# First layer norm of a transformer block: the transposes of tiles 8 to 15 move from TensorE to the DMA queue, and the order of work is planned anew

## The chip, the cores and the metric

One core of a Trainium2 chip. Its engines work in parallel, each through a list of instructions of its own, in order: PE (TensorE, matmuls), ACT (ScalarE), DVE (VectorE), POOL (GpSimd) and SP (SyncE, which issues nearly all DMAs here). An instruction waits at the head of its list until the semaphores that it names have come up, and all behind it wait too. The metric is the device time of one execution in microseconds, the median of several runs. The profile is one more execution, recorded instruction by instruction; its times count from the start of the recorded span.

## The reference

One adaptive layer-norm transformer block over 2048 tokens of width 1024: attention with 32 query heads that share one key and one value head of width 32, then a gated feed-forward layer of width 3584. Cut to what is computed:

```python
mod = (silu(c) @ w_mod).reshape(1, 6, 1, -1)
sa, ca, ga, sb, cb, gb = (mod[:, i] for i in range(6))
h = layernorm(x) * (1 + ca) + sa
q = heads(h @ wq)                       # 32 heads of width 32
k, v = h @ wk, h @ wv                   # one head each
p = softmax(q @ k.T * 32 ** -0.5)
x = x + ga * (concat(p @ v) @ wo)
h = layernorm(x) * (1 + cb) + sb
x = x + gb * ((silu(h @ w1) * (h @ w3)) @ w2)
```

## The kernel before

The tokens are cut in 16 tiles of 128 (index `tt`) and in 8 blocks of 256 (index `n`). TensorE contracts over partitions, so the normed input must lie with its features on partitions: that is `HT`, 128 x 8 x 2048, and the first norm fills it tile by tile.

**First norm, `lnt1(tt)`.** Per tile: two statistics instructions and an aggregation on VectorE (`ST`, `MV`), two or three tiny instructions on GpSimd (`RS`, `NB`), then the norm itself into one of three slots `XN[tt % 3]` (`XNB` 0, `XNB` 1 and a slice of `PS`), on ScalarE for tiles 0 to 7 and on VectorE from tile 8 on. Then TensorE transposes the slot in eight 128 x 128 pieces into a PSUM bank, and ScalarE or VectorE (whichever the planner picks) copies the bank into `HT`. A slot can be written again when its transposes are done. Tiles 6 to 15 of x lie in the buffer `W2S`.

**Projections.** `k_proj(j)` takes `HT` tiles 2j and 2j+1, eight matmuls, and its result goes into `KT` part j (by VectorE or ScalarE). `v_proj(tb)` takes four tiles, 32 small matmuls. `q_proj` fills `QT`. `mod_chunk(i)` loads 1 MB of `w_mod` into one of two buffers inside `W2S` and multiplies it with silu(c).

**Attention.** One step c stands for block n, query group f (of 8) and key part j (of 8): `s_exp(c)` issues 8 score matmuls (S) on TensorE and two exponentials on ScalarE (U<-S), each 128 x 1024. There are 512 steps, so 1024 exponentials. Step c of the first row (c = 0 to 7) needs `KT` part c. `av` multiplies U with V and sums the denominators; `wo` adds the attention output to x and takes the second norm; `slab` and `quarter` are the feed-forward layer (a tanh on ScalarE per slab). In the second norm of blocks 1 to 6 the transposes are already done by DMA, SBUF to SBUF (`wo`, `dma_start_transpose` from `XN` into `QT`).

**Order.** Nothing above fixes the order on an engine. `Graph` collects the operations with their dependencies, a due time `vt` and an estimated duration; `Placer.run` then simulates the engines, and picks at each point among the operations that are ready. `PLAN` has one row for 16 steps: tolerances, and offsets to the due times by kind and engine (`"k/dve"`). What `Placer` picks becomes the fixed list of each engine. `Placer.commit` books the estimated end of an operation. For a DMA it books one shared queue, `self.bw`: a transfer starts when the earlier ones are through, takes `nbytes / n.bw`, and ends 0.5 later in the planner's account.

**The lists around the change, before.** e3 is one of the two exponentials of step 3, S3 its matmuls, T and N the transposes and the norm of a tile, H its copy into `HT`, k4 the matmuls of `k_proj(4)`, KT4 its eviction. From the first exponential on:

```
ACT: e0 e0 e1 e1 H11 e2 e2 e3 KT5 H12 e3 e4 H13 e4 H14 e5 H15 e5 e6 KT7 e6 e7 e7 ...
PE:  S0 q T9 S1 T10 k2 T11 S2 k3 k4 S3 k5 T12 S4 qbias T13 S5 T14 k6 T15 vbr S6 v0 k7 v1 S7 v2 v3 S8 ...
DVE: ... N11 QT H9 H10 KT2 ... KT3 KT4 N12 ... N13 ... N14 ... N15 KT6 ...
SP:  ... x(8-11) w_mod w_mod wq x(12-15) WO WO w_mod(0) w_mod(1) ...
```

T8 stands on TensorE ahead of S0, and H8 on ScalarE ahead of e0. SP's load of WO waits until wq has landed.

Of the kernel before, what the change touches and what calls it, by code (L numbers as in the profile page):

```python
# [8 lines left out]
P = 128  # L9
# [33 lines left out]
class Graph:  # L43
# [63 lines left out]
    def alias(self, new, old):  # L107
# [5 lines left out]


PLAN = [
    (0.2, 0.03, 0.0, 0, 1.4,
     {"q/pe": -9, "slab/act": -80, "wo/dve": -71, "ln/pe": -112, "ln/act": 31, "k/pe": 3, "k/dve": 33}),
    (0.0, 0.12, 0.2, 1, 0.2,
     {"av/pe": -2, "q/pe": -9, "pair/dve": -2, "av/dve": -33, "slab/act": -18, "ln/pe": -57, "ln/act": 23}),
    (0.0, 0.16, 0.02, 0, 0.7, {"wo/pe": 106, "q/pe": -45, "q/dve": -74, "ln/pe": -118, "ln/dve": 4, "mod/pe": -24}),  # L120
    (0.0, 0.16, 0.02, 0, 0.7, {"wo/pe": 106, "q/pe": -45, "q/dve": -74, "ln/pe": -118, "ln/dve": 4, "mod/pe": -24}),
    (0.2, 0.24, 0.2, 1, 0.6, {"q/pe": 47, "mc/pe": 46, "ln/act": -12, "k/pe": 22}),
    (0.0, 0.12, 0.2, 0, 1.8,
     {"wo/pe": -44, "quarter/pe": 47, "q/pe": 33, "mc/pe": 36, "pair/dve": -14, "wo/dve": -1, "ln/act": -12,
      "k/pe": 22}),
    (0.0, 0.11, 0.2, 1, 1.5, {"q/pe": 47, "mc/pe": 46, "av/dve": 6, "ln/act": -12, "k/pe": 22}),
    (0.0, 0.11, 0.2, 1, 1.9, {"q/pe": -13, "mc/pe": 46, "av/dve": 4, "ln/act": -12, "k/pe": 22}),
    (0.0, 0.11, 0.2, 0, 3.4, {"wo/pe": 35, "an/dve": 55, "slab/dve": 1}),
    (0.0, 0.11, 0.2, 1, 1.4, {"av/dve": -11, "an/dve": 55, "slab/dve": 1, "q/dve": 9}),
    (0.0, 0.11, 0.1, 0, 2.4,  # L130
     {"wo/pe": 14, "slab/pe": 12, "quarter/pe": 3, "q/pe": -6, "av/dve": 18, "an/dve": 69, "slab/act": -1,
      "quarter/dve": -7}),
    (0.0, 0.11, 0.05, 0, 2.4, {"slab/act": 6, "wo/dve": 53}),
    (0.0, 0.11, 0.2, 0, 2.9, {"wo/pe": 46, "an/dve": 55, "slab/dve": -89, "q/dve": 67}),
    (0.0, 0.11, 0.2, 1, 1.3, {"wo/pe": -13, "pair/dve": 6, "an/dve": 55, "slab/dve": -89, "q/dve": 67}),
    (0.0, 0.11, 0.1, 1, 2.7,
# [16 lines left out]
     {"wo/pe": 112, "slab/pe": -124, "quarter/pe": 26, "q/pe": 20, "mc/pe": 46, "pair/dve": 13, "av/dve": -89,  # L153
      "an/dve": -26, "slab/dve": -39, "slab/act": -20, "quarter/dve": 35, "wo/dve": -2, "ln/act": -12,
      "k/pe": 22}),
    (0.0, 0.11, 0.2, 1, 1.3,
     {"slab/pe": -124, "quarter/pe": 26, "q/pe": 52, "mc/pe": 46, "pair/dve": 13, "av/dve": -72, "an/dve": -26,
      "slab/dve": -39, "slab/act": -20, "quarter/dve": 35, "wo/dve": -6, "ln/act": -12, "k/pe": 22}),
    (0.0, 0.11, 0.05, 1, 2.6,
     {"slab/pe": -124, "quarter/pe": 26, "q/pe": 20, "mc/pe": 46, "av/dve": -89, "slab/dve": -39,  # L160
      "slab/act": -20, "quarter/dve": 35, "ln/act": -12, "k/pe": 22}),
    (0.0, 0.11, 0.05, 1, 1.4,
     {"slab/pe": -124, "quarter/pe": 26, "q/pe": 20, "mc/pe": 5, "av/dve": -89, "slab/act": -20,
      "quarter/dve": 35, "ln/act": -12, "k/pe": 22}),
    (0.0, 0.11, 0.2, 0, 1.6, {"wo/pe": 74, "pair/dve": 40, "av/dve": -2, "an/dve": 55, "slab/dve": -102, "q/dve": 6}),
    (0.0, 0.11, 0.2, 1, 1.4, {"wo/pe": -13, "pair/dve": 40, "av/dve": -2, "an/dve": 55, "slab/dve": -88}),
    (0.0, 0.11, 0.05, 1, 1.9,
# [19 lines left out]
class Placer:  # L187
# [121 lines left out]
    def commit(self, n, e, k, start):  # L309
        eng, fn, dur = n.alts[k]  # L310
        e = eng
        s = n.sess
        if s is not None and s.bank is None:
            bt, b = self.bank_for(n)
            s.bank = b
            s.prev = self.bank_of[b][1]
            self.bank_of[b] = None
            for p in s.prev:
                n.preds.setdefault(p, False)
        n.eng = e  # L320
        if e == "sp" or n.dma is not None:
            self.t[e] = start + dur
            self.bw = max(self.bw, start + 2.6) + n.nbytes / n.bw
            n.fin = self.bw + 0.5
        else:
            if e == "dve" and n.tag in ("pair", "av"):
                self.lock = start + dur
            if e == "pool" and self.lock > start:
                dur = max(dur, self.lock - start + (0.43 if dur > 0.5 else 0.1))
            self.t[e] = start + dur  # L330
            n.fin = start + dur + n.post + self.SEM
        if e == "pe":
            if s is not None and n.mode == "F":
                s.fill = any(not x.done and x is not n and x.alts[0][0] == "pe" for x in s.nodes)
                if s.fill:
                    self.fills.add(s)
                else:
                    self.fills.discard(s)
            if n.mode == "S":
                self.step += 1  # L340
            self.mode = n.mode
            if n.mode != "S":
                self.run_of = n.mode
            else:
                self.t_s = self.t["pe"]
        n.done = True
        if s is not None:
            s.left -= 1
            if s.left == 0:
                users = [x for x in s.nodes if x.eng != "pe"] or [s.nodes[-1]]  # L350
                self.bank_of[s.bank] = (max(x.fin for x in users), tuple(users))
        self.emit(n, e, fn)
        self.free_pending()
# [90 lines left out]
def build(nc, x_in, wq_in, wk_in, wv_in, wo_in, w1_in, w3_in, w2_in, c_in, wmod_in, out, S, D, F):  # L444
    G = Graph(nc)
    op = G.op
    NC = D // P
# [21 lines left out]
    HT = sb("HT", [P, NC, S], BF16)  # L469
# [38 lines left out]
    XN = [XNB[:, 0], XNB[:, 1], PS[:, 5].rearrange("p h q -> p (h q)")]  # L508
    o = 0
# [19 lines left out]
    def xtile(tt):  # L529
        if tt < 6:  # L530
            return X1[:, tt // 2, tt % 2, :]
        return W2f[:, (tt - 6) * D:(tt - 5) * D]

    def xkey(tt):
        return [("X", tt // 2, tt % 2, q) for q in range(4)] if tt < 6 else [("XS", tt)]
# [56 lines left out]
    def wq_dma(f0, f1, key, vt):  # L592
# [18 lines left out]
       writes=["C1"], vt=-1990)  # L611
    op("dve", lambda: [lambda e: e.tensor_scalar(SCC[:, 2, :], SCC[:, 1, :], 0.5, 0.5, ALU.mult, ALU.add)], 0.17,
       reads=["C1"], writes=["C2"], vt=-1990)
    op("dve", lambda: [lambda e: e.tensor_tensor(SCC[:, 3, :], SCC[:, 2, :], SCC[:, 0, :], ALU.mult)], 0.17,
       reads=["C0", "C2"], writes=["C3"], vt=-1990)
# [11 lines left out]
    for i in range(2):  # L627
# [3 lines left out]
           writes=[("S", 4)], vt=-1990, mode="F", post=0.145, waw=(i == 0))  # L631
# [5 lines left out]
       reads=[("WKV", 0)], writes=["WKR0"], vt=-1600)  # L637
# [13 lines left out]
    def ln_norm(xap, tt, keys, slot, vt):  # L651
        op("dve", lambda: [lambda e: e.tensor_scalar(XN[slot], xap, MV[:, tt, 0:1], RS[:, tt:tt + 1],
                                                     ALU.subtract, ALU.mult)], 0.455,
           reads=keys + [("MV", tt), ("RS", tt)], writes=[("XN", slot)], vt=vt)

    def lnt1(tt, vt):
        G.tag = "ln"
        slot = tt % 3
        xap = xtile(tt)
        ln_stats(xap, tt, xkey(tt), vt)  # L660
        if tt < 8:
            op("pool", lambda: [lambda e: e.tensor_scalar(NB_[:, tt:tt + 1], MV[:, tt, 0:1], RS[:, tt:tt + 1], -1.0,
                                                          ALU.mult, ALU.mult)], 0.3, reads=[("MV", tt), ("RS", tt)],
               writes=[("NB", tt)], vt=vt)
            op("act", lambda: [lambda e: e.activation(XN[slot], xap, ACT.Identity, bias=NB_[:, tt:tt + 1],
                                                      scale=RS[:, tt:tt + 1])], 1.15,
               reads=xkey(tt) + [("RS", tt), ("NB", tt)], writes=[("XN", slot)], vt=vt)
        else:
            ln_norm(xap, tt, xkey(tt), slot, vt)
        static = tt < 6  # L670
        s = None if static else Sess()
        bk = [("S", tt)] if static else [("sess", id(s), tt)]

        def tr(b=tt):
            return [lambda e, cc=cc: e.transpose(
                BANKH[b][:, cc * P:(cc + 1) * P], XN[slot][:, cc * P:(cc + 1) * P],
                IDENT[:]) for cc in range(NC)]
# [547 lines left out]
```

## Time and profile before

| what | us |
|---|---|
| median of 3 runs (lowest, highest) | 1134.34 (1134.11, 1134.49) |
| profiled execution, its own time | 1134.47 |
| its span | 1132.6 |
| PE busy | 1113.1 |
| ACT busy | 1026.0 |
| DVE busy | 951.9 |
| POOL busy | 53.8 |
| first exponential starts | 30.61 |
| ACT idle, 300 to 400 / 400 to 500 | 0 / 1.4 |

The busy time of an engine is the union of its instructions' times; matmuls overlap, so a busy TensorE is not one at its peak. A group's line names the output tile, the input tiles, shapes and count, then busy us and mean ns of one, then the engine's idle us just before such instructions and who ended it. In a timeline the columns are start, length, engine, instruction; neighbours of one kind are merged, with their count at the end. The granted TensorE clock was 1.00 in all stretches.

### The profile page before, as it was taken

How to read it: one execution, taken by the hardware profiler on the slowest of the kernel's cores; microseconds unless marked ns; L12 is line 12 of the kernel's file. 1: busy time of each engine (PE TensorE's matmuls, PEld its weight loads, DVE VectorE, ACT ScalarE, POOL GpSimd, SP SyncE). 2: the span in 40 equal slices, each digit the busy share in tenths (PEclk: the TensorE clock that was granted, in tenths of full speed). 3: DMA queues.
4: the chain of work that ended last, by engine and by line, in shares of the span. 5: the costliest groups of instructions: out<-in, count | busy, mean ns of one | idle time of the engine just before them, and what ended most of it. 6: DMA issues, size and time to landing. Idle time of an engine off the chain costs nothing.

```text
span 1132.6 us, 34805 instructions
## 1 busy us (share of the span) xinstructions
PE 1113.1 (98%) x15600; PEld 754.6 (67%) x15600; DVE 951.9 (84%) x1544; ACT 1026.0 (91%) x1165; POOL 53.8 (5%) x95
## 2 busy tenths in 40 slices
PE   7999999999999999999999999999999999999998
PEld 6643546666577656776567756776577657766887
DVE  7888899989988888888988998888988988888442
ACT  6999999999999999999999999999999999996110
POOL 5100000000100001000100000000100000000000
PEclk9999999999999999999999999999999999999999
DMA  9500379665596667766596658765696559667793
GB/s 344 184 2 1 114 225 242 186 196 151 129 263 194 173 166 209 208 191 165 141 262 192 174 148 237 196 193 142 173 248 195 160 146 238 190 185 209 217 296 116
DMA packets 374292, 209.47 MB, mean 185 GB/s; under 512 B 17536, under 2 KB 365952, under 8 KB 374144
## 3 DMA queue, kind: packets, MB, share of 16 engines
q1 hardware_dynamic: 373712, 207.11, 65.8%
q8 instruction: 123, 2.02, 0.8%
q14 instruction: 25, 0.20, 0.1%
q10 hardware_dynamic: 432, 0.13, 0.0%
HBM read 199.89 MB, written 4.19 MB: 180 GB/s over the span
## 4 chain that ended last, share of the span: by engine, by line
PE 63%; ACT 31%; DVE 4%; DMA 1%; issue 0%; POOL 0%; SPq 0%; DVEq 0%
PE PB L22 47%; ACT U L22 30%; PE S L22 16%; DVE PS L22 2%; DMA W<-in_A_wq_dram 1%; ACT HT L22 1%; DVE HT L22 1%; DVE RB L22 0%; SPq L22 0%; DVE ST L22 0%; DVE W L22 0%; ACT XNB L22 0%; POOL PS L22 0%; DVE XNB L22 0%; POOL RS L22 0%
## 5 line engine op out<-in xcount | busy, mean ns | idle before, releaser
L22 ACT ACTIVATE U<-S 128x1024 bf16<-128x1024 f32 x1024 | 964.3, 1111 | 9.0 <-PE S L22 8.8
L22 DVE TENSOR_TENSOR PS<-U 128x2048 bf16<-128x2048 bf16 x256 | 309.7, 1214 | 11.7 <-ACT U L22 10.3
L22 DVE TENSOR_TENSOR PS<-PS 128x1024 bf16<-128x1024 bf16 x368 | 249.5, 684 | 4.7
L22 PE MATMUL PB<-QT,W 128*128 128x256 bf16 x1856 | 229.6, 273 | 0.0
L22 PE MATMUL S<-QT,KT 32*128 32x256 bf16 x4096 | 203.5, 273 | 6.0 <-ACT U L22 4.0
L22 PEld LDWEIGHTS PB<-QT,W 128*128 128x128 bf16 x1856 | 170.3, 98 | 46.6 <-issue 28.3
L22 PE MATMUL PB<-W2S,HT 128*128 128x256 bf16 x1512 | 189.1, 273 | 0.0
L22 PEld LDWEIGHTS PB<-W2S,HT 128*128 128x128 bf16 x1512 | 137.5, 98 | 42.4 <-issue 26.4
L22 PEld LDWEIGHTS S<-QT,KT 32*128 32x128 bf16 x4096 | 60.8, 92 | 132.7 <-ACT U L22 118.7
L22 PE MATMUL PB<-U,V 128*32 128x256 bf16 x4032 | 123.5, 273 | 0.0
L22 PE MATMUL PB<-QT,HT 128*128 128x256 bf16 x960 | 119.9, 273 | 0.0
L22 PEld LDWEIGHTS PB<-U,V 128*32 128x32 bf16 x4032 | 100.8, 97 | 18.8 <-issue 7.0
L22 ACT ACTIVATE HT<-PB 128x512 bf16<-128x512 f32 (+1 forms) x110 | 77.6, 707 | 32.0 <-PE PB L22 31.8
L22 PEld LDWEIGHTS PB<-QT,HT 128*128 128x128 bf16 x960 | 88.2, 98 | 23.7 <-issue 14.1
L22 PE MATMUL PB<-HT,W 128*128 128x256 bf16 (+1 forms) x576 | 101.8, 318 | 1.0 <-DVE HT L22 0.6
L22 DVE SCALAR_TENSOR_TENSOR HT<-HT,PB 128x512 bf16<-128x512 bf16 x102 | 69.4, 681 | 34.2 <-ACT HT L22 33.4
L22 DVE TENSOR_TENSOR HT<-HT,PB 128x512 bf16<-128x512 bf16 x102 | 69.5, 681 | 19.2 <-PE PB L22 18.5
L22 PEld LDWEIGHTS PB<-HT,W 128*128 128x128 bf16 x576 | 49.9, 97 | 38.1 <-issue 15.2
L22 DVE STREAM_TRANSPOSE RB<-PB 128x256 f32<-128x256 f32 x63 | 28.2, 448 | 38.7 <-PE PB L22 38.5
L22 PE MATMUL PB<-WO,QT 128*128 128x512 bf16 x232 | 57.3, 381 | 0.0
L22 POOL TENSOR_SCALAR RS<-MV 128x1 f32<-128x1 f32 x32 | 10.5, 329 | 969.9 <-DVE MV L22 966.9
L22 ACT ACTIVATE HT<-S 128x512 bf16<-128x512 f32 (+1 forms) x15 | 10.9, 736 | 30.5 <-PE S L22 30.5
(115 smaller groups left out, 675.2 us busy)
## 6 DMA issues: line engine op xcount, KB each, us to landing
W<-in_B_w_dram SPq DMA_DIRECT2D x150, 512.0 KB, 4.8
W2S<-in_B_w_dram SPq DMA_DIRECT2D x28, 1792.0 KB, 8.6
HT<-in_B_w_dram SPq DMA_DIRECT2D x74, 512.0 KB, 4.8
W2S<-in_w_mod_dram SPq DMA_DIRECT2D x8, 1024.0 KB, 7.2
X<-in_A_x_dram SPq DMA_DIRECT2D x8, 512.0 KB, 7.0
out_dram<-X SPq DMA_DIRECT2D x7, 512.0 KB, 9.1
U<-in_B_w_dram SPq DMA_DIRECT2D x1, 3584.0 KB, 13.5
W2S<-in_B_w_dram SPq DMA_DIRECT2D x1, 3584.0 KB, 15.2
```

The costliest lines, as they stand in the source:

```text
L22: return getattr(e, call[0])(*call[1], **call[2])
```

## The change

In `lnt1`, tiles 8 to 15 leave the function early: in place of eight TensorE transposes, a PSUM bank and a copy there is one `dma_start_transpose` on SP, from the norm's slot straight into `HT`. Its rate is given as a negative number, and `Placer.commit` has a branch for it: such a transfer neither waits for the shared queue `self.bw` nor adds to it. Tiles 0 to 7 stay as they were. `PLAN` has new values in rows 0 to 11 and in two later rows, so the lists of all engines differ in many places.

```diff
-    (0.2, 0.03, 0.0, 0, 1.4,
-     {"q/pe": -9, "slab/act": -80, "wo/dve": -71, "ln/pe": -112, "ln/act": 31, "k/pe": 3, "k/dve": 33}),
...
+    (0.0, 0.15, 0.1, 0, 2.9,
+     {"slab/pe": -44, "q/pe": 25, "mc/pe": 25, "slab/dve": -38, "slab/act": -18, "wo/dve": -95, "ln/pe": -112,
+      "ln/act": 172, "k/dve": 33, "v/pe": 7, "mod/pe": 109, "kb/pe": -5, "mc/dve": 47}),
...
         if e == "sp" or n.dma is not None:
             self.t[e] = start + dur
-            self.bw = max(self.bw, start + 2.6) + n.nbytes / n.bw
-            n.fin = self.bw + 0.5
+            if n.bw < 0:
+                n.fin = start + 2.6 - n.nbytes / n.bw + 0.5
+            else:
+                self.bw = max(self.bw, start + 2.6) + n.nbytes / n.bw
+                n.fin = self.bw + 0.5
...
             ln_norm(xap, tt, xkey(tt), slot, vt)
+        if tt >= 8:
+            o = op("sp", lambda: [lambda e: e.dma_start_transpose(HT[:, :, tt * P:(tt + 1) * P], XN[slot])], 0.5,
+                   reads=[("XN", slot)], writes=[("HT", cc, tt) for cc in range(NC)], vt=vt, dma=("HTL", slot), nbytes=1 << 18)
+            o.bw = -262144.0 / 1.0 * 1.0
+            return
         static = tt < 6
```

The lists around it in the changed program, T now being a DMA on SP (which waits for its norm), and N11 waiting on VectorE until T8 has read the shared slot (N12 for T9, and so on):

```
ACT: e0 e0 e1 KT3 e1 KT4 e2 e2 KT5 e3 e3 e4 e4 e5 e5 KT6 e6 e6 KT7 e7 e7 ...
PE:  S0 q k2 S1 k3 k4 S2 qbias k5 S3 vbr S4 v0 S5 v0 v1 v2 k6 S6 mc0 k7 v3 S7 q S8 ...
DVE: N8 N9 N10 SAB QBI QT QT N11 KT2 ... N12 ... N13 ... QBI VBR WQ N14 WQ N15 V0 WQ V1 ...
SP:  ... x(8-11) w_mod w_mod wq x(12-15) T8 T9 T10 WO WO w_mod(0) T11 w_mod(1) T12 T13 T14 T15 w_mod(2) ...
```

Ahead of e0 there are small moves too: the copy of tile 1 goes from ScalarE to VectorE, one copy of the k and v weights' set-up goes the other way and one back.

More of the change, by code (lines that the diff above doesn't have):

```diff
@@ L115 @@
 PLAN = [
-    (0.2, 0.03, 0.0, 0, 1.4,
-     {"q/pe": -9, "slab/act": -80, "wo/dve": -71, "ln/pe": -112, "ln/act": 31, "k/pe": 3, "k/dve": 33}),
[L118 to L133, printed above, removed]
+    (0.0, 0.15, 0.1, 0, 2.9,
+     {"slab/pe": -44, "q/pe": 25, "mc/pe": 25, "slab/dve": -38, "slab/act": -18, "wo/dve": -95, "ln/pe": -112,
+      "ln/act": 172, "k/dve": 33, "v/pe": 7, "mod/pe": 109, "kb/pe": -5, "mc/dve": 47}),
@@ new lines @@
+    (0.0, 0.11, 0.1, 1, 1.6,
+     {"slab/pe": -44, "q/pe": 25, "mc/pe": 74, "an/dve": 48, "slab/dve": -38, "slab/act": -106, "wo/dve": -95,
+      "q/dve": 55, "ln/pe": -112, "ln/act": 172, "k/dve": 33, "v/pe": 7, "mod/pe": 109, "kb/pe": -5,
+      "mc/dve": 47}),
+    (0.0, 0.15, 0.1, 0, 0.7, {"wo/pe": 106, "q/pe": -78, "q/dve": -74, "ln/pe": -118, "ln/dve": 4, "mod/pe": -24}),
+    (0.0, 0.15, 0.1, 0, 0.7, {"wo/pe": 106, "q/pe": -78, "q/dve": -74, "ln/pe": -118, "ln/dve": 4, "mod/pe": -24}),
@@ new lines @@
+    (0.0, 0.15, 0.1, 0, 0.7, {"q/pe": 82, "ln/pe": -118, "ln/dve": 4, "mod/pe": -24}),
+    (0.0, 0.14, 0.2, 1, 1.5,
+     {"av/pe": 11, "wo/pe": -44, "quarter/pe": 47, "pair/dve": -2, "wo/dve": 2, "ln/act": -12, "k/pe": 22}),
+    (0.0, 0.14, 0.1, 1, 1.5,
+     {"av/pe": 11, "wo/pe": -44, "quarter/pe": 47, "pair/dve": -2, "wo/dve": 2, "ln/act": -12, "k/pe": 22}),
+    (0.0, 0.13, 0.2, 0, 2.8, {"wo/pe": 14, "quarter/pe": 3, "q/pe": -6, "av/dve": 18, "an/dve": 69}),
+    (0.0, 0.12, 0.2, 1, 4.3, {"wo/pe": 15, "quarter/pe": -92, "q/pe": -6, "av/dve": 18}),
@@ L134 @@
+    (0.0, 0.12, 0.2, 1, 3.4, {"wo/pe": 15, "quarter/pe": 51, "q/pe": -6, "av/dve": 18}),
+    (0.0, 0.11, 0.2, 1, 1.4, {"q/pe": -13, "mc/pe": 46, "wo/dve": 29, "ln/act": -12, "k/pe": 22}),
+    (0.0, 0.11, 0.2, 0, 2.4, {"quarter/pe": -10, "slab/act": 6, "wo/dve": 53}),
     (0.0, 0.11, 0.2, 0, 2.9, {"wo/pe": 46, "an/dve": 55, "slab/dve": -89, "q/dve": 67}),
@@ L155 @@
       "k/pe": 22}),
-    (0.0, 0.11, 0.2, 1, 1.3,
-     {"slab/pe": -124, "quarter/pe": 26, "q/pe": 52, "mc/pe": 46, "pair/dve": 13, "av/dve": -72, "an/dve": -26,
+    (0.0, 0.11, 0.2, 1, 1.4,
+     {"slab/pe": -124, "quarter/pe": 26, "q/pe": 52, "mc/pe": 46, "pair/dve": 13, "av/dve": 56, "an/dve": -26,
       "slab/dve": -39, "slab/act": -20, "quarter/dve": 35, "wo/dve": -6, "ln/act": -12, "k/pe": 22}),
@@ L161 @@
       "slab/act": -20, "quarter/dve": 35, "ln/act": -12, "k/pe": 22}),
-    (0.0, 0.11, 0.05, 1, 1.4,
-     {"slab/pe": -124, "quarter/pe": 26, "q/pe": 20, "mc/pe": 5, "av/dve": -89, "slab/act": -20,
-      "quarter/dve": 35, "ln/act": -12, "k/pe": 22}),
+    (0.0, 0.11, 0.1, 1, 2.4,
+     {"wo/pe": 37, "slab/pe": -124, "quarter/pe": 26, "q/pe": 20, "mc/pe": 56, "pair/dve": -74, "av/dve": -89,
+      "an/dve": -26, "slab/dve": 6, "slab/act": -20, "quarter/dve": 35, "wo/dve": 10, "ln/act": -12, "k/pe": 22}),
     (0.0, 0.11, 0.2, 0, 1.6, {"wo/pe": 74, "pair/dve": 40, "av/dve": -2, "an/dve": 55, "slab/dve": -102, "q/dve": 6}),
```

## The prediction

> **What bounds the kernel now.** I read three things in this order: who is busy over the whole span, who waits for whom, and then the first 60 us instruction by instruction, because the eight tiles of the change live there. The costliest group of the page is ScalarE's softmax exponential (U<-S):
>
> ```profile
> L22 ACT ACTIVATE U<-S 128x1024 bf16<-128x1024 f32 x1024 | 964.3, 1111 | 9.0 <-PE S L22 8.8
> ```
>
> All 1024 of them together were held up only 9.0 us. The timeline of ScalarE at the other end shows where they stop and what follows:
>
> ```profile
> 1029.02 7.48 ACT L22 ACTIVATE U<-S 128x1024 bf16<-128x1024 f32 x8
> 1057.87 0.60 ACT L22 ACTIVATE HT<-PB 128x512 bf16<-128x512 f32 x1 [21.37 <-PE PB L22]
> ```
>
> The last exponential ends at 1029.02 + 7.48 = 1036.5; the 96.1 us from there to the span's end (1132.6) are matmuls of the last block, which ScalarE waits for. So the time is: start of the first exponential (30.6), plus a stream in which ScalarE is nearly always busy, plus a tail on TensorE. TensorE's 98% busy is no second bound inside the stream: its weight loads for S wait 118.7 us for U, that is, for ScalarE. A microsecond by which ScalarE idles in the stream is a microsecond of the end. Here is its timeline at the front (start, length, instruction):
>
> ```profile
> 30.24 0.47 ACT L22 ACTIVATE KT<-PB,QKB 128x256 bf16<-128x256 f32 x1 [0.63 <-PE PB L22]
> 30.61 3.76 ACT L22 ACTIVATE U<-S 128x1024 bf16<-128x1024 f32 x4
> 34.28 1.02 ACT L22 ACTIVATE HT<-PB 128x1024 bf16<-128x1024 bf16 x1
> 35.20 3.10 ACT L22 ACTIVATE U<-S 128x1024 bf16<-128x1024 f32 x3
> ...
> 41.42 1.04 ACT L22 ACTIVATE HT<-PB 128x1024 bf16<-128x1024 bf16 x1
> 42.33 1.06 ACT L22 ACTIVATE U<-S 128x1024 bf16<-128x1024 f32 x1
> ...
> 46.01 1.96 ACT L22 ACTIVATE U<-S 128x1024 bf16<-128x1024 f32 x2
> 47.82 0.51 ACT L22 ACTIVATE KT<-PB,QKB 128x256 bf16<-128x256 f32 x1
> 48.17 27.73 ACT L22 ACTIVATE U<-S 128x1024 bf16<-128x1024 f32 x30
> ```
>
> No gap after 30.6. An exponential takes 0.917 of ScalarE in a row (34.28 - 30.61 for four), an HT copy 0.91, a KT 0.35 to 0.45 (0.4 below). Thirteen exponentials start before 48.17, so number 17, the first of step 8, starts at 48.17 + 3 x 0.917 = 50.9. That is the mark I compare at.
>
> The queue of loads (timeline of SP, then the DMA rows of windows that hold one issue each, last column us from issue to landing: the X load at 16.70, the WO load at 30.23, the w_mod load at 31.19):
>
> ```profile
> 16.70 5.47 SPq L22 DMA_DIRECT2D W2S<-in_A_x_dram  x1
> 30.23 0.92 SPq L22 DMA_DIRECT2D WO<-in_A_wo_dram  x2
> 31.19 3.37 SPq L22 DMA_DIRECT2D W2S<-in_w_mod_dram  x2
> ```
>
> ```profile
> W2S<-in_A_x_dram SPq DMA_DIRECT2D x1, 1024.0 KB, 16.0
> WO<-in_A_wo_dram SPq DMA_DIRECT2D x1, 1024.0 KB, 5.6
> W2S<-in_w_mod_dram SPq DMA_DIRECT2D x1, 1024.0 KB, 10.4
> ```
>
> They land at 32.7, 35.8 and 41.6: in the order of issue, each waiting its turn, about 3.0 us per MB (41.6 - 32.7 = 8.9 for the two WO halves and the first w_mod chunk, 1 MB each). And one transpose by DMA of the kind that the kernel already has later on (window 295 to 300, nothing else in flight):
>
> ```profile
> q1 hardware_dynamic: 1056, 0.26, 27.3%
> QT<-XNB SPq DMA_TRANSPOSE x1, 3.1
> ```
>
> It goes through q1, the queue of all the loads; it lands 3.1 us after issue, and holds the engines for 27.3% of 5 us = 1.36 us. All twelve of them run so, with the queue empty. Last, TensorE's pieces that I need:
>
> ```profile
> 46.71 1.03 PE L22 MATMUL PB<-HT,PS 128*128 128x256 bf16 x8
> 48.47 0.40 PE L22 MATMUL S<-QT,KT 32*128 32x256 bf16 x8
> 48.80 1.59 PE L22 MATMUL PB<-PS,HT 128*128 128x32 bf16 x56
> ```
>
> A k projection is 1.03, an S step 0.33 to the next matmul, and the v matmuls 0.028 each.
>
> **The change part by part.** I write T8 to T15 for the transposes of tiles 8 to 15, N8 to N15 for their norms on VectorE, k4 to k7 for the k projections of tiles (8,9) to (14,15), KT4 to KT7 for their evictions, e3 for the two exponentials of step 3.
>
> Removed: 64 TensorE transposes (72 of them are 5.5 us busy, so 76 ns each, 4.9 us), two VectorE copies (0.69 each), six ScalarE copies, one before the first exponential and five in the stream: 5 x 0.91 = 4.6 us of the bound engine. Added on ScalarE: KT3, KT4 and KT6, which VectorE did before, 3 x 0.4 = 1.2. If nothing waited, the mark would move by -3.4. Added on SP: eight issues of 1.24 (median of the twelve), and on the queue eight times 1.36.
>
> Now the waits. T8, T9, T10 can be issued when their norms are done. In the trace of before these stand at 24.9 to 27.6 and nothing ahead of them on VectorE changes by more than one statistics instruction (0.6). SP is idle from 22.2 to 30.2, so the issue is hidden. But the queue then still holds the loads of wq and of x that land at 30.2 and 32.7. In turn: T8 at 32.7 + 1.36 = 34.1, T9 at 35.4, T10 at 36.8.
>
> N11 writes the slot that T8 reads, so on VectorE it waits until 34.1 (29.57 before). Behind it on that engine stand KT2 and the statistics of tiles 12 to 15. KT2 must end for k4, k4 also needs T9: it starts at 35.5, KT4 on ScalarE at 36.6. ScalarE's own row reaches KT4 at 30.6 + 4 x 0.917 + 0.4 = 34.7. It idles 1.9, then runs KT4 and e2 until 38.9.
>
> T11 is issued at about 34.6 (N11 takes 0.5). SP has by then passed the two WO loads and the first w_mod chunk, 8.9 us of queue: 36.8 + 8.9 + 1.36 = 47.0. k5 follows on TensorE with S of step 3 behind it, KT5 on ScalarE with e3 behind it: k5 47.1 to 48.1, KT5 to 48.5, e3 from 48.5. ScalarE idles 9.2. The cover that would hide a late T11 is gone by construction: no exponential stands between KT5 and e2.
>
> The rest of the row: behind T11 the second w_mod chunk (3.0), so T12 to T15 land at 51.4, 52.7, 54.1, 55.5. e3 to e5 run until 48.5 + 6 x 0.917 = 54.0. S of step 5 waits for the first half of e4 (48.5 + 2 x 0.917 + 1.11 = 51.4); behind it 80 v matmuls (2.2) and k6 (1.03): 51.4 + 0.33 + 2.2 + 1.03 = 55.0, KT6, e6 from 55.5. ScalarE idles 1.1. TensorE goes on with S of step 6 (to 55.4), 32 matmuls of mc (a later chunk's took 1.16: 56.6), k7 (T15 is there: 57.6), 32 v matmuls (0.9: 58.5) and S of step 7 (58.9). e7 starts at 58.9, step 8 at 58.9 + 1.83 = 60.8. Against 50.9: **+9.9**.
>
> Of the other edits: the first exponential shifts by between -0.6 and +0.6 (T8's eight matmuls and copy are gone from the chain to it, one statistics instruction of 0.6 stands ahead of SAB on VectorE); I take 0. After step 8 the instructions of ScalarE are the same in number (1008 exponentials, 98 tanh in the stream, 14 after it), and TensorE has the same 418 groups after the last S, so the tail stays 96.1. The stalls of before there are six of 1.36, one of 0.48 and one of 0.16; the last five of 1.36 lie 126.2 apart, one per block, where only two rows of the plan differ. What is open to the new order is thus some 2.0 us, gained or given: I take 0 and keep both ends.
>
> Sum: 1134.5 (profiled execution, span 1132.6 and 1.9 around it) + 9.9 = 1144.4; the median of the runs is 0.1 below the profiled one: **1144.3**.
>
> Two rules bear on this. The Trainium skill, "DMA: Bandwidth & Descriptors", section "Two DMAs through the same engine are not ordered", says that descriptors of one queue start in order; the loads above agree, and no row of before shows a transpose behind loads. By that rule the sum stands as it is. The Trainium skill, "Advanced Engine Details and Errata", section "X-Bar Transpose (TRN2)", puts such transposes at 350 to 400 GB/s; the row has 0.26 MB in 1.36 us, 190 GB/s. By the page's rate, as an estimate, each would hold the queue for 0.7, T11 would land 2.6 earlier and the sum would be 1141.7.
>
> The queue share of one transpose is the unknown that matters. Its lowest bound is nothing: T11 then lands at 32.7 + 8.9 = 41.6, which is 5.4 earlier, and the sum is 1138.9. Its upper bound is the whole 3.1 (the second rival). Near the row, with 0.7 to 2.0, the first gives 2.6 less (1141.7); with 2.0 T15 lands at 60.6 and leads: k7 to 61.7, v 0.9, S 0.4, e7 at 63.0, step 8 at 64.9, 1148.4.
>
> **The rivals.** *The transposes pass the loads* (other side). If a transpose took 3.1 whatever is queued, T9 would be there at 30, T11 at 33.2 (N11 at 29.6), and it decides as soon as T11 lands by 35.8, when ScalarE calls for k5. Then ScalarE alone would be 3.4 ahead, but the TensorE row behind step 5 leads: first half of e4 done at 30.6 + 9 x 0.917 + 3 x 0.4 + 0.2 = 40.3, + 0.33 + 2.2 + 1.03 = 43.9 for k6, then S 0.33, mc 1.16, k7 1.03, v 0.9, S 0.4: e7 at 47.7, step 8 at 49.5, 1.4 less than 50.9. That gives 1132.9; with nothing of TensorE's row in the way 1130.9. For it speaks only that the changed planner reckons so (a negative rate leaves the shared queue untouched); against it the landing order and that both kinds use q1.
>
> *A transpose does not overlap its neighbours*: each holds the queue for its whole 3.1. T10 42.0, T11 54.0, T15 69.4, k7 to 70.5, e7 at 71.8, step 8 at 73.6: +22.7, 1157. For it: no row shows two in a row without a gap. Against: the loads overlap (5.6 alone against 3.0 per MB in turn).
>
> **How the numbers follow.** In turn as in the sum: 0.80, own range 1138.9 to 1149. Passing the loads: 0.12. No overlap: 0.08. The range for 8 in 10 reaches from 1137 (the lowest of the likeliest case and 2.0 from the new order after step 8) to 1151; it leaves out most of both rivals. Less than 0.2% (2.3 us) can't be told from no change. Slower by more: the likeliest and the second rival, less a little: 0.86. Within: 0.08, faster: 0.06, both from the first rival, whose 1132.9 lies within and whose best end 1130.9 beyond.
>
> **What would show it.** DMA rows HT<-XNB and HT<-PS with a median near 8 us from issue to landing in place of 3.1; SP's transpose of tile 11 issued near 35 and landing near 47; one gap of about 9 us on ScalarE ahead of a KT near 48, waiting for TensorE, which waits for the DMA; step 8 near 61; the last exponential to the end still 96 us. I am wrong if the transposes land about 3 us after issue, if the gap lies elsewhere, or if the stream after step 8 changes by more than 2 us.

## The result and the profile after

The changed kernel takes 1147.01 us (median of 4 runs, 1146.67 to 1147.44) against 1134.41 for the kernel before in the same session (1134.11 to 1134.67): a ratio of 1.0111, 95% interval 1.0094 to 1.0129. It is 12.6 us slower.

The profile says where. ScalarE's exponentials first, on the page of the changed kernel, then two rows of its timeline near the end (start, length):

```profile
L22 ACT ACTIVATE U<-S 128x1024 bf16<-128x1024 f32 x1024 | 963.3, 1106 | 11.6 <-PE S L22 9.7
```

```profile
1026.23 23.15 ACT L22 ACTIVATE U<-S 128x1024 bf16<-128x1024 f32 x25
1070.74 0.60 ACT L22 ACTIVATE HT<-PB 128x512 bf16<-128x512 f32 x1 [21.37 <-PE PB L22]
```

The exponentials cost what they did, and were themselves held up only 2.6 us more. The last row of 25 starts at 1026.23; in the kernel before it starts at 1013.35. It is 12.9 late, and what follows is equal: the end of this row is 96.0 before the end of the span (1145.4), and 96.1 in the kernel before. So the time was lost ahead of it. Here is the front (ScalarE's timeline of the changed kernel):

```profile
30.55 2.99 ACT L22 ACTIVATE U<-S 128x1024 bf16<-128x1024 f32 x3
33.48 0.47 ACT L22 ACTIVATE KT<-PB,QKB 128x256 bf16<-128x256 f32 x1
33.85 1.01 ACT L22 ACTIVATE U<-S 128x1024 bf16<-128x1024 f32 x1
38.41 0.47 ACT L22 ACTIVATE KT<-PB,QKB 128x256 bf16<-128x256 f32 x1 [3.54 <-PE PB L22]
38.96 1.94 ACT L22 ACTIVATE U<-S 128x1024 bf16<-128x1024 f32 x2
48.86 0.47 ACT L22 ACTIVATE KT<-PB,QKB 128x256 bf16<-128x256 f32 x1 [7.96 <-PE PB L22]
49.42 5.61 ACT L22 ACTIVATE U<-S 128x1024 bf16<-128x1024 f32 x6
56.93 0.47 ACT L22 ACTIVATE KT<-PB,QKB 128x256 bf16<-128x256 f32 x1 [1.91 <-PE PB L22]
58.12 1.94 ACT L22 ACTIVATE U<-S 128x1024 bf16<-128x1024 f32 x2 [0.72 <-PE S L22]
60.09 0.47 ACT L22 ACTIVATE KT<-PB,QKB 128x256 bf16<-128x256 f32 x1
61.22 9.42 ACT L22 ACTIVATE U<-S 128x1024 bf16<-128x1024 f32 x10 [0.66 <-PE S L22]
```

The rows KT are KT3 to KT7. The row without a gap is gone: 3.54 idle ahead of KT4, 7.96 ahead of KT5, 1.91 ahead of KT6. Step 8 starts two exponentials after 61.22, at 61.22 + 1.83 = 63.05, against 50.9: **12.15 of the 12.9**. The other 0.7 lies between step 8 and the last row.

Why KT5 is late: TensorE had nothing to give it. TensorE's timeline, and SP's (where the length of a DMA row is the time that its issue held SP):

```profile
32.39 1.05 PE L22 MATMUL PB<-HT,PS 128*128 128x256 bf16 x8
36.94 1.42 PE L22 MATMUL PB<-HT,PS 128*128 128x256 bf16 x8 [3.50 <-DMA HT<-XNB]
...
46.93 1.89 PE L22 MATMUL PB<-HT,PS 128*128 128x256 bf16 x8 [5.59 <-DMA HT<-PS]
...
55.03 1.87 PE L22 MATMUL PB<-HT,PS 128*128 128x256 bf16 x8
```

```profile
25.79 3.21 SPq L22 DMA_TRANSPOSE HT<-PS  x1
29.06 5.04 SPq L22 DMA_TRANSPOSE HT<-XNB  x2
34.14 2.00 SPq L22 DMA_DIRECT2D WO<-in_A_wo_dram  x2
36.18 0.66 SPq L22 DMA_DIRECT2D W2S<-in_w_mod_dram  x1
36.88 6.12 SPq L22 DMA_TRANSPOSE HT<-PS  x1
```

k3, k4, k5 and k6 stand there in this order; k5 waited for the DMA of tile 11, issued at 36.88. The DMA row of that issue alone has 10.0 us to landing:

```profile
HT<-PS SPq DMA_TRANSPOSE x1, 10.0
```

It lands at 46.9, right behind w_mod(0), issued at 36.18 and landed at 46.1. And the same eight matmuls took 1.05 as k3, 1.89 as k5 and 1.87 as k6. The windows of the changed kernel show why (the third number from the right is the granted clock of TensorE; the first after the comma is its busy time):

```profile
37.00:41.00 4.00, 4.00 (x59) 3.04 (x60) 4.00 (x11) 2.41 (x3) 1.65 (x5) 0.57 1.06 386
41.00:47.00 6.00, 0.41 (x13) 0.29 (x10) 0.66 (x3) 0.00 (x0) 1.49 (x4) 0.77 1.11 352
47.00:58.00 11.00, 9.02 (x152) 5.48 (x152) 5.97 (x14) 6.55 (x8) 0.00 (x0) 0.50 0.78 170
```

After each long wait TensorE worked for a stretch at half its clock: k4 took 1.42 while the clock fell, k5 and k6 stood in the slow stretch whole. In the kernel before, the clock was 1.00 in all stretches.

### The profile page after: what moved, and what is told of

Its sections match the earlier page's. It is cut to its first block, busy times and chain, and to the rows that moved or that the text cites. A ratio compares the mean times of both kernels' runs of the same rounds, so it can differ in the third digit from the quotient of the medians.

```text
span 1145.4 us, 34645 instructions
## 1 busy us (share of the span) xinstructions
PE 1112.2 (97%) x15506; PEld 752.3 (66%) x15536; DVE 949.1 (83%) x1540; ACT 1021.9 (89%) x1161; POOL 51.6 (5%) x95
## 4 chain that ended last, share of the span: by engine, by line
ACT 59%; PE 33%; DVE 4%; DMA 3%; issue 0%; SPq 0%; DVEq 0%; ACTq 0%
ACT U L22 56%; PE PB L22 23%; PE S L22 10%; ACT HT L22 4%; DMA HT<-PS 2%; DVE PS L22 1%; DMA W<-in_A_wq_dram 1%; DVE ST L22 1%; DMA QT<-XNB 0%; DVE HT L22 0%; DVE X L22 0%; SPq L22 0%; DVE QT L22 0%; DVE RB L22 0%; DVE MV L22 0%
## 5 line engine op out<-in xcount | busy, mean ns | idle before, releaser
L22 DVE TENSOR_TENSOR PS<-U 128x2048 bf16<-128x2048 bf16 x256 | 309.7, 1215 | 12.2 <-ACT U L22 11.3
L22 PEld LDWEIGHTS S<-QT,KT 32*128 32x128 bf16 x4096 | 60.8, 92 | 137.2 <-ACT U L22 123.6
L22 PE MATMUL PB<-HT,W 128*128 128x256 bf16 (+1 forms) x561 | 98.0, 316 | 3.4 <-issue 1.4
L22 DVE SCALAR_TENSOR_TENSOR HT<-HT,PB 128x512 bf16<-128x512 bf16 x102 | 69.5, 682 | 35.6 <-ACT HT L22 35.1
L22 ACT ACTIVATE HT<-PB 128x512 bf16<-128x512 f32 (+1 forms) x104 | 71.1, 684 | 30.8 <-PE PB L22 30.8
L22 PEld LDWEIGHTS PB<-HT,W 128*128 128x128 bf16 x576 | 50.3, 98 | 37.7 <-issue 13.6
L22 PE MATMUL PB<-WO,QT 128*128 128x512 bf16 x217 | 53.8, 380 | 1.6 <-issue 0.9
```

The source lines that it names most:

```text
L22: return getattr(e, call[0])(*call[1], **call[2])
```

## The experiments

Each run has its own runs of the kernel before beside it (medians 1134.34 to 1134.80). "Mark" is the start of step 8: 50.9 before, 63.05 changed.

**1. The loads behind the transposes.** SP's list alone is changed:

```diff
-SP: T8 T9 T10 WO WO w_mod(0) T11 w_mod(1) T12 T13 T14 T15
+SP: T8 T9 T10 T11 w_mod(0) T12 T13 T14 T15 WO WO w_mod(1)
```

> Every list but SP's is that of the changed kernel; on SP the two WO loads and the second w_mod load are issued after the transpose of tile 15, and the first w_mod load right behind the transpose of tile 11. Theory 'in turn' (a transpose waits in the queue for every load issued before it): nothing stands between the transposes of tiles 10 and 11 any more, so tile 11 lands near 39.3 in place of 46.9, the 8.0 us gap of ScalarE before KT5 shrinks to under 1 us, step 8 starts near 53 in place of 63.1, and the time falls by 9 to 11 to 1136-1138, still not below the kernel before, because tiles 8 to 10 stay behind the x and wq loads. Rival 'the transposes are slow by themselves' (their issue on SP took 3.2 to 6.1 us in the changed kernel): tile 11 lands no earlier than some 3 us before 46.9 and the time stays at 1144-1149.

1141.23 (ratio 1.0054, 1.0038 to 1.0071), mark 57.5. T11 landed at 38.5 instead of 46.9, T12 to T15 at 44.1, 45.0, 47.9, 49.8. That is the queue in turn: T11 came even 0.8 earlier than the theory said (39.3), where the rival had it at 44 or later. But the time did not fall to 1136 to 1138, nor step 8 to 53: on these the theory was wrong. 5.8 of the 12.6 are the place of these four loads; KT4 to KT7 still waited 3.29, 1.38, 1.57 and 1.58, and the clock was low twice. Runs 3 and 6 take this up.

**2. One load more ahead of T11.** The opposite dose: w_mod(1) goes ahead of T11 too.

```diff
-SP: ... WO WO w_mod(0) T11 w_mod(1) T12 ...
+SP: ... WO WO w_mod(0) w_mod(1) T11 T12 ...
```

> As the changed kernel, but the second w_mod load (1 MB) is issued ahead of the transpose of tile 11 too, not behind it. Theory 'in turn': tile 11 lands one MB later, 46.9 + 3.0 = 49.9, tiles 12 to 15 as before, and the wait of k5 passes on whole to the end: 1147.0 + 3.0 = 1150. Rival 'slow by themselves': the landing of tile 11 and the time do not change, 1147.

1150.75 (1.0140, 1.0125 to 1.0155): T11 at 49.7, 2.8 later for 1 MB more and again 0.8 behind the last load, the wait at KT5 10.48 instead of 7.96. With run 1 this settles it: T11 waits its turn in the queue.

**3. TensorE kept busy in the changed kernel.** 28 matmuls of the identity behind k3 and 44 behind q's bias, into banks that are free.

```diff
-PE: ... k3 k4 S2 qbias k5 ...
+PE: ... k3 [28] k4 S2 qbias [44] k5 ...
```

> As the changed kernel, with 28 matmuls of 128x256 on the identity (3.1 us, result never read) on TensorE behind k3 and 44 (4.8 us) behind the q bias matmuls, so that TensorE is busy while it waits for the transposes of tiles 9 and 11. Theory 'clock': in the changed kernel the granted clock was 0.50 from about 37.3 to 40.7 and from 44.2 to 57.8, which stretched k5, k6 and the matmuls between; with TensorE kept busy the clock stays at 1.00, the landing of tile 11 stays near 46.9, the start of step 8 goes from 63.1 to about 61, and the time falls by 1.8 to 2.5 to about 1144.8. Rival: the clock costs nothing because all waits are for the DMA: 1147.

1147.92 (1.0116, 1.0101 to 1.0131): no gain. k4 was at 1.05 and q's bias at 1.66, so the first slow stretch was gone, but T11 came 1.4 later in this kernel (48.3), and w_mod(0) ahead of it 1.3 later (47.4; why is open), TensorE was idle 3.63 ahead of k5 in spite of the filling, and the clock was 0.50 behind it as before. This run doesn't tell the clock's share.

**4. The transposes on another queue.** ScalarE issues the eight transposes; nothing else is changed.

```diff
-o = op("sp", lambda: [lambda e: e.dma_start_transpose(HT[:, :, tt * P:(tt + 1) * P], XN[slot])], ...
+o = op("act", lambda: [lambda e: e.dma_start_transpose(HT[:, :, tt * P:(tt + 1) * P], XN[slot])], ...
```

> As the changed kernel, but ScalarE issues the eight transposes, on its own DMA queue, at the places where the planner had them on SP. Theory 'in turn, per queue': in another queue they need not wait for SP's loads; each lands within 3 to 6 us of its issue, tile 11 near 36; no gap of ScalarE is longer than 2 us; the price is the issue on ScalarE, five of them in the stream at 1.24 = 6.2, so the time lies near 1134.5 - 3.4 + 6.2 and some stalls on TensorE's row, 1137 to 1141. Rival 'in turn at the engines' (the 16 DMA engines serve all queues in the order of issue): tile 11 lands near 47 as before and ScalarE waits as long, with the issues on top: 1148 to 1154.

1151.45 (1.0147, 1.0132 to 1.0162): the rival's time (1148 to 1154) was right, and a queue of their own doesn't bring the transposes in early. ScalarE's timeline:

```profile
26.12 1.33 ACTq L22 DMA_TRANSPOSE HT<-PS  x1
27.49 3.86 ACTq L22 DMA_TRANSPOSE HT<-XNB  x1
31.40 1.02 ACT L22 ACTIVATE HT<-PB 128x1024 bf16<-128x1024 bf16 x1 [4.53 <-issue]
...
37.74 5.72 ACTq L22 DMA_TRANSPOSE HT<-PS  x1
43.51 1.02 ACT L22 ACTIVATE U<-S 128x1024 bf16<-128x1024 f32 x1 [6.18 <-DVE ST L22]
```

T8 landed at 33.9, T9, issued at 27.49, at 40.2, T10 at 47.0 and T11, issued at 37.74, at 50.8. Beside loads in the other queue they come 6.3, 6.8 and 3.7 apart. It isn't strictly the order of issue, as the rival had it: T11 landed ahead of w_mod(1), which was issued at 32.12 and landed at 52.7; from 40 on, transfers of the two queues landed mixed (T9, both halves of WO, T10, w_mod(0), T11, w_mod(1)). The issue itself holds ScalarE up to 5.72, and the first exponential starts at 35.4 instead of 30.5, so the total has this price in it too. The last row's releaser is named as DVE; ScalarE was in the issue until 43.46.

**5. The plan alone, the move alone.** The code before with the new rows; the changed code with the old rows.

> The kernel before with the changed plan rows, every transpose on TensorE. Theory (the move sets the loss, not the search): the first exponential stream has no wait for a DMA transpose, step 8 starts within 1.5 us of 50.9. Rival (the new rows by themselves spread the first steps): step 8 later than 56. The total isn't a measure of either, since the rows from about the sixteenth on were found for other lists of work: anywhere from 1134 to 1160.

> The changed kernel with the plan rows of before: eight tiles transposed by DMA, placed by rows found for transposes on TensorE. Theory (the move sets the loss): step 8 starts at 58 to 66, as the transposes stand behind or beside the same loads. Rival (the new rows cause it): step 8 before 54. The total lies above that of the run with the new rows alone by about the difference of the two marks, if the rest is spoilt alike in both; it may not be.

With the rows alone step 8 starts at 49.9, 1.0 earlier than before; with the move alone at 61.9. ScalarE's timeline of the move alone, around its long wait:

```profile
42.22 4.67 ACT L22 ACTIVATE U<-S 128x1024 bf16<-128x1024 f32 x5
55.43 0.47 ACT L22 ACTIVATE KT<-PB,QKB 128x256 bf16<-128x256 f32 x1 [8.53 <-PE PB L22]
```

The long wait is at KT6 here, not at KT5: with these rows all four loads stand behind T11, and T12 and T13 landed at 52.4 and 53.4 behind them. The move, not the new rows, makes the loss at the front; which key part waits depends on the rows. The totals are no measure of it: 1181.3 and 1182.1 (1.0411, 1.0390 to 1.0431, and 1.0417, 1.0397 to 1.0438). The 12 us between their marks are gone by the last exponentials (rows start at 1055.29 and 1055.34), and the last exponential is 121 and 120 from the end instead of 96: rows found for one list of work spoil another from front to tail. The guess that the totals would differ as the marks do was wrong.

**6. Run 1 with TensorE kept busy.** 28 identity matmuls behind k3, and the score matmuls of steps 3 to 5 three times each, the same values into the same bank. The transfers stay where they are.

```diff
-PE: ... k3 k4 S2 qbias k5 S3 vbr S4 ... S5 ...
+PE: ... k3 [28] k4 S2 qbias k5 S3 S3 S3 vbr S4 S4 S4 ... S5 S5 S5 ...
```

> The run with the loads behind T11 and T15 (1141.2), with TensorE kept busy: 28 matmuls of the identity behind k3, and the score matmuls of steps 3, 4 and 5 issued three times (the same values again, into the same bank). No transfer is moved. Theory (the granted clock of 0.5 after TensorE had too little to do is what k4, k6, mc and k7 lost): k4 1.03 instead of 1.39, k6 1.04 instead of 1.87, mc 1.17 instead of 1.89, k7 1.04 instead of 1.90; T12 to T15 land where they did (44.1 to 49.8); step 8 at 55.0 to 56.0 instead of 57.5, total 1139.0 to 1140.0. Rival (the transfers alone set the stage, the slow clock is hidden under them): step 8 at 57.2 to 57.8, total 1140.9 to 1141.6.

1138.75 (1.0034, 1.0021 to 1.0048), 2.5 less than run 1 from more work. The windows of run 1 and of this run:

```profile
41.00:47.70 6.70, 4.98 (x140) 3.80 (x138) 3.68 (x12) 5.40 (x7) 1.54 (x4) 1.00 0.99 152
47.70:54.50 6.80, 6.23 (x77) 4.47 (x74) 4.89 (x13) 2.97 (x4) 0.00 (x0) 0.51 0.94 277
```

```profile
41.00:47.70 6.70, 5.23 (x173) 4.17 (x171) 4.20 (x14) 6.08 (x7) 1.86 (x4) 1.00 1.17 191
47.70:54.50 6.80, 6.23 (x123) 4.34 (x119) 6.61 (x16) 4.59 (x7) 0.00 (x0) 1.00 1.10 269
```

The clock stays at 1.00, k6 takes 1.03 (1.87 in run 1) and k7 1.03 (1.90), and step 8 starts at 54.8 instead of 57.5, though T12 to T15 landed up to 1.3 later than in run 1 (45.3, 46.3, 47.3 and 50.7, three of the four). So the clock cost some 2.7 there: the theory held, with mark and total a little below its ranges.

**7. The order put right.** If the loss is only that each engine meets the transposes too early in its list, another order must cure it, with nothing added or taken away. (VectorE's list moves along: KT2 and the copies of q's and v's bias stand earlier; the product mc goes behind step 16.)

```diff
-SP:  T8 T9 T10 WO WO w_mod(0) T11 w_mod(1) T12 T13 T14 T15
+SP:  T8 T9 T10 T11 T12 T13 T14 T15 w_mod(0) WO WO w_mod(1)
-ACT: e0 e0 e1 KT3 e1 KT4 e2 e2 KT5 e3 e3 e4 e4 e5 e5 KT6 e6 e6 KT7 e7 e7
+ACT: e0 e0 e1 KT3 e1 e2 e2 e3 KT4 e3 e4 KT5 e4 e5 e5 KT6 e6 e6 KT7 e7 e7
-PE:  S1 k3 k4 S2 qbias k5 S3 vbr S4 v0 S5 v0 v1 v2 k6 S6 mc k7 v3 S7 ...
+PE:  S1 k3 S2 qbias vbr S3 k4 S4 k5 S5 v0 v1 v2 k6 S6 k7 S7 v3 ...
```

> The changed kernel with another order in the first 55 us, nothing added or taken away: both WO loads and both w_mod loads go behind T15 on SP's queue; k4 to k7 stand on TensorE and ScalarE just ahead of the step that first reads their keys (e2 and e3 no longer stand behind KT4 and KT5); q's bias and v's go before the waits; the one product that reads w_mod(0) goes behind step 16. Theory (the loss is the wait for T8 to T15 in the order in which ScalarE meets them, and nothing after step 8): T8 to T11 as in the run with the loads behind T11 (34.6, 37.0, 37.8, 38.5), T12 to T15 with no load ahead of them at about 42.4, 43.6, 45.5 and 46.2; ScalarE waits some 1 us at KT4 and 2 to 3 us at KT6, and step 8 starts at 51 to 52 instead of 63.05; total 1147.0 - 12 = 1135, range 1133.5 to 1138. Rival (the changed plan loses time behind step 8, or transposes are slow by themselves): step 8 at 51 to 55, total 1139 to 1145.

1142.7 (1.0064, 1.0047 to 1.0080). At the mark it came near what the theory asked for (51 to 52): step 8 at 53.2, with T12 to T15 at 43.1, 45.0, 46.5 and 47.8, 0.7 to 1.6 later than reckoned, as VectorE took the statistics of tile 12 at 36.1 though its x was there at 32.5. But TensorE's granted clock fell here too (a window of this run, then a row of TensorE's timeline):

```profile
43.30:56.90 13.60, 11.18 (x114) 5.67 (x115) 9.32 (x18) 6.62 (x9) 0.09 (x1) 0.50 0.98 294
```

```profile
53.02 4.67 PE L22 MATMUL PB<-HT,W 128*128 128x512 bf16 x12
```

k6 and k7 took 1.87 and 1.89. ScalarE then waited 2.90 and 1.37 for score matmuls: in my order the 12 q matmuls of this row stood between two of them, and the product that reads w_mod(0) had been put into a full step. The 12 took 4.67, most of it at half the clock; in run 8 eight take 1.90 at 1.00. The executions differ in the same way: the one with a mean clock of 0.999 took 1140.19, the three with 0.994 to 0.996 took 1142.57 to 1143.04. So mark and total lie in the rival's ranges (51 to 55, 1139 to 1145), but not for its reasons: what the trace shows as lost are the late statistics, the clock and my own order behind step 8.

**8. The same, mended.** The statistics as soon as x is there, and fewer products between score matmuls.

```diff
-DVE: QT KT2 N11 qbias vbr st12 st12 st13 ... N12 ... N13 ...
+DVE: QT KT2 st12 st12 N11 st13 st13 qbias vbr st14 N12 st14 N13 ...
-PE:  ... v0 v1 v2 k6 S6 k7 S7 v3 S8 (12 q) S9 ...
+PE:  ... v0 v1 k6 S6 v2 k7 v3 S7 (4 q) S8 (8 q) S9 ...
```

> The kernel with the steps in time (1142.7), with its three lapses mended; nothing added or taken away against the changed kernel. (1) VectorE takes the statistics of tiles 12 to 15 as soon as their x is there (32.6) instead of behind the copies of q's bias and v's (36.1), and TensorE does k6 before v's third quarter. (2) The score matmuls of steps 8 to 10 get their places back, so that no more than four q products stand between two of them (there 12 stood between steps 8 and 9: ScalarE waited 2.90). (3) The product that reads w_mod(0) goes behind step 13, and the q products behind it are shifted so that each step keeps about 1.6 us of TensorE's work (there ScalarE waited 1.37). Theory (the loss lies in the order around the transposes, not in the transposes): T8 to T11 at 34.4, 36.8, 37.6, 38.3 as there; T12 to T15 issued at 37.6, 38.9, 40.2, 41.5 and landed 3.3 later each, at 40.9, 42.2, 43.5, 44.8; ScalarE waits some 0.2 at KT6, 0.7 for S6 and 0.7 for S7; step 8 starts at 49.2 (48.7 to 50.5) instead of 63.05; behind it as in the changed kernel; total 1147.0 - 13.8 = 1133.2, range 1132.0 to 1135.0. Rival (the transposes by themselves cannot be in time, or TensorE's clock falls again as it waits for them): step 8 at 51.5 or later, total 1136 to 1139.

1140.19 (1.0050, 1.0036 to 1.0064), above the ranges of theory and rival. ScalarE's timeline at step 7 and step 8:

```profile
48.17 1.94 ACT L22 ACTIVATE U<-S 128x1024 bf16<-128x1024 f32 x2 [0.60 <-PE S L22]
50.89 1.94 ACT L22 ACTIVATE U<-S 128x1024 bf16<-128x1024 f32 x2 [0.78 <-PE S L22]
```

ScalarE is done with step 7 at 50.1; step 8 starts at 50.9, 12.2 earlier than in the changed kernel and level with the kernel before. (The next expectation's 50.0 is the end of step 7, not the start of step 8.) The clock is 1.00 throughout. So eight transposes by DMA can be in time: the waits at KT4 to KT7 are 0.18, none, 1.01 and none. From step 8 to step 14, however, ScalarE waited 5.0 for score matmuls, while TensorE waited 1.58 for q's weights, which VectorE scales, and 1.48 for a bank that VectorE empties.

Two more runs shifted work in those steps. In the first, q's weights are scaled ahead of the pair sums and score matmuls are moved ahead where a step is overfull; in the second, only up to about step 18.

> The kernel with the statistics early (1140.2), whose transposes were all in time (step 8 at 50.0) and whose ScalarE then waited 5.0 us for score matmuls in steps 8 to 16. Again nothing added or taken away: VectorE scales all eight parts of wq before the first pair sum (the q products of step 8 waited 1.58 for the last of them); the product with w_mod(0) stands ahead of the first denominators instead of behind them (it waited 1.48 for their bank); and from step 8 on a score matmul is moved ahead wherever the work since the last one would exceed what a step holds. Theory (with the transposes in time, what is left is TensorE's order in steps 8 to 16): step 8 at 49.5 to 50.1, ScalarE's waits for score matmuls from there to 70 us together 0.5 to 1.5 instead of 5.0, total 1140.2 - 4.0 = 1136.2, range 1134.8 to 1137.5; about level with before, and not under it, as the changed rows behind step 16 wait 0.9 us more than those of before. Rival (TensorE is short of time in these steps, since its idle time while it waits for keys can't be made up): the waits stay at 3.5 or more, total 1138.5 to 1140.5.

> The last kernel (1140.8) waited 1.04 us in steps 8 to 16 as expected, but score matmuls were also moved past the U products of steps 18 to 46, and ScalarE waited 4.1 us there for them. Here only steps 8 to 18 are touched, and from about step 18 on TensorE's order is that of the changed kernel again; the q evacuation of step 9 on VectorE goes ahead of one sum that TensorE does not wait for. Nothing is added or taken away. Theory (the loss lies in the order in which the engines meet the transposes; put right, it is gone): step 8 at about 49.7, ScalarE's waits for score matmuls from there to 135 us 0.8 to 1.8 instead of 5.1, total 1140.8 - 3.8 = 1137.0, range 1135.0 to 1138.0: the changed kernel's +12.6 cut to +2.5, of which 0.9 are the waits that the changed rows have behind step 16 in any case. Rival (TensorE is short of time in these steps): waits of 3.5 or more, total 1139 to 1141.

The first took 1140.77 (1.0056, 1.0042 to 1.0069): the waits in steps 8 to 16 fell to 1.04 as expected, but the total did not (1136.2 was expected), as 4.1 came up behind them, where score matmuls had been moved past the products with U. The second took 1137.75 (1.0030, 1.0017 to 1.0042), the best of the versions with the move, and as expected (1137.0). Its timeline of ScalarE, from KT4 on:

```profile
38.04 0.47 ACT L22 ACTIVATE KT<-PB,QKB 128x256 bf16<-128x256 f32 x1 [0.24 <-PE PB L22]
...
44.59 0.47 ACT L22 ACTIVATE KT<-PB,QKB 128x256 bf16<-128x256 f32 x1 [1.15 <-PE PB L22]
45.57 1.94 ACT L22 ACTIVATE U<-S 128x1024 bf16<-128x1024 f32 x2 [0.51 <-PE S L22]
...
48.61 5.61 ACT L22 ACTIVATE U<-S 128x1024 bf16<-128x1024 f32 x6 [0.66 <-PE S L22]
54.42 4.01 ACT L22 ACTIVATE U<-S 128x1024 bf16<-128x1024 f32 x4 [0.21 <-PE S L22]
```

Of the waits of 3.54, 7.96 and 1.91, 0.24, none and 1.15 are left; step 8 starts at 48.61 + 1.83 = 50.4. Yet it is 3.3 slower than the kernel before. From the mark to the last 25 exponentials (1016.51) it takes 966.1, the changed kernel 963.2 and the kernel before 962.5. Of the 2.9 over the changed kernel, 2.1 are idle time of ScalarE (12.0 against 9.9 in that stretch), 1.7 of it listed by its timeline between 54 and 72 us; the rest isn't located. And of the 3.4 that the prediction counted as saved on ScalarE, most is waited away ahead of the mark (0.24, 1.15, 0.51 and 0.66). No version with the move beat the kernel before.

## Why the prediction was right

| step of it | predicted | measured |
|---|---|---|
| T8, T9, T10 land | 34.1, 35.4, 36.8 | 34.5, 36.9, 37.7 |
| KT4 starts, ScalarE idle ahead of it | 36.6, 1.9 | 38.4, 3.54 |
| T11 lands | 47.0 | 46.9 |
| issue to landing, median | near 8 | 5.2 (HT<-XNB), 8.7 (HT<-PS) |
| k5, KT5 done | 48.1, 48.5 | 48.8, 49.3 |
| T12 to T15 land | 51.4, 52.7, 54.1, 55.5 | 50.7, 51.7, 54.5, 55.6 |
| k6 done, e6 starts | 55.0, 55.5 | 56.9, 58.1 |
| e7, step 8 | 58.9, 60.8 | 61.2, 63.05 |
| behind step 8 to the last row | 0 within 2.0 | +0.7 |
| tail | 96.1 | 96.0 |

The forecast was 1144.3 with a range of 1137 to 1151, and slower at 0.86; the measured 1147.0 lies inside. The main mechanism held: the transposes stand in the loads' queue, T11 comes behind 3 MB of loads, and k5, KT5 and e3 wait for it one behind the other. Run 1 moved T11 ahead of all three loads, run 2 behind one more, and the time followed; run 5 gave the loss at the front to the move alone.

That T11 is met within 0.1 is in part luck. T8, T9 and T10 landed 1.8, 2.4 and 0.8 behind what stood ahead of them, not 1.36 each; the three loads took 8.4, not 8.9; T11 came 0.8 behind the last. So T10 was 0.9 late, and the rest made it up. T14 and T15 were met by another path than the prediction's, which had them in the queue behind T13. VectorE's timeline of the changed kernel:

```profile
49.82 0.19 DVE L22 COPY VBR<-PB 128x32 f32<-128x32 f32 x1 [8.16 <-PE PB L22]
...
50.32 0.54 DVE L22 TENSOR_SCALAR PS<-W2S,MV,RS 128x1024 bf16<-128x1024 bf16 x1
```

The norm of tile 14 (the second row) stood behind the copy of v's bias, which waited 8.16 for a product that TensorE does behind k5. So T14 was issued only at 50.89, and it landed 2.9 behind T13: its issue was the bound, not the queue.

The first rival (the transposes pass the loads) is out: T11 took 10.0 us, and even a queue of its own gained nothing. The second (no overlap, 3.1 each) is out as well: without loads between them T10 and T11 come 0.8 and 0.7 behind their forerunners in run 1. By the Trainium skill, "DMA: Bandwidth & Descriptors", section "Two DMAs through the same engine are not ordered", descriptors of one queue start in order; T11 at 46.9 behind w_mod(0) at 46.1 agrees.

Mis-sized was TensorE's own time after the waits: the prediction took 1.03 for each k projection, "k5 47.1 to 48.1" and k6 likewise, from a row at a granted clock of 1.00. At 0.50 they took 1.89 and 1.87. KT5 and e3 came 0.9 later by that, and k6 was done 1.9 late.

One dependency was left out as well. The prediction has "S of step 6 (to 55.4)" right behind k6, done at 55.0; but S of step 6 reads KT6, and TensorE waited for ScalarE's eviction:

```profile
57.46 0.61 PE L22 MATMUL S<-QT,KT 32*128 32x256 bf16 x8 [0.57 <-ACT KT L22]
```

With the wait of 0.57, and 0.61 for S instead of 0.40, S of step 6 was done 2.7 late, at 58.07. What follows, with the clock at 1.00 again, took some 0.4 less than reckoned, so the mark was missed by 2.25. With the 0.7 behind the mark this makes up the 2.7 between 1144.3 and 1147.0 to within 0.3. That the clock costs time in such a stage was shown in run 6 (2.7), but in the order of run 1, not in that of the changed kernel, where run 3 failed to keep the clock up.

Two smaller errors cost nothing. T9 came 2.4 behind T8, not 1.36, and no run says why; for that and for k4's 1.42 the wait at KT4 was 1.6 longer, but e2 was done at 40.9, long before T11. And T8 to T11 held SP 3.21, 3.45, 1.54 and 6.12 us by their issue instead of 1.24 each, and T11 was issued at 36.9, not 34.6; w_mod(0) landed only at 46.1, so the queue was the later bound for T11 all the same.

That the cover "is gone by construction", because KT4 and KT5 stand ahead of e2 and e3, was the other part of the cause: KT4 is first read in step 4 and KT5 in step 5. Run 7 put them to where they are read, and T8 to T11, which landed as in run 1, cost 0.2 there instead of 3.29 and 1.38.

## What to carry to other kernels

A transfer of 0.26 MB that takes 3 us on an empty queue takes 10 behind 3 MB of loads; reckon its landing from what is ahead of it in the queue, and in a planner book it on the same queue as the loads. Where work is moved to a slower path, look in each engine's list for what stands behind the first reader: moving four loads took back 5.8 of the 12.6 us, and lists in the order of first use brought the whole stage back to its old length (step 8 at 50.4 to 50.9). The total stayed 3.3 us above the kernel before even so, as the new order cost time behind that stage. And where TensorE waits, look at the granted clock of that stretch before taking a matmul's time from another: here eight matmuls took 1.87 to 1.89 instead of 1.03.

## What was not expected of the hardware

**Half the clock without a long gap.** In the changed kernel the granted clock fell to 0.50 right after an idle time of 3.50 and within one of 5.59. The Trainium skill, "TensorE: Matmul & The Clock Gate", section "HAM oscillation — how this bites in real kernels", warns of idle gaps over about 3.4 us; these two agree. In run 2 the clock was at 0.50 from 35.6 on, within an idle time of only 3.10 (TensorE's row at 36.74). And in run 1 the warning doesn't cover what was seen: the clock was 0.51 from 47.7 on, though no gap in the 6.7 us ahead was over 0.94 and TensorE was busy for 4.98 of them. The same page's section "A second HAM failure mode: psum-queue depth-cycling" has short idle times between groups lower the clock, and this fits better; that it is the cause isn't shown. With 5.23 of the 6.7 us busy, in run 6, it stayed at 1.00; where the limit lies, and whether busy time is the measure, these runs don't say.

**An issue that holds its engine.** A transpose's issue takes 1.24 us on an empty queue, and in the changed kernel T8 to T13 held SP for 1.5 to 6.1; on ScalarE's queue it was up to 5.72 (run 4). The three loads between T10 and T11 took 0.6 to 1.4 each. But loads can do it too: the last load of x held SP 5.47 in the kernel before.

**A second queue makes it worse.** On ScalarE's queue, beside the loads on SP's, T9 and T10 landed 6.3 and 6.8 behind their forerunners, against 0.8 and 0.7 for T10 and T11 in run 1. The loads came later too: the first half of WO landed at 42.6, against 35.8 in the kernel before.
